# Stretched routing steps, whole-row second matrices of four experts and outputs in columns of 256, 128 and 128, in an attention, GLU and soft-MoE kernel

## The chip, the cores and the metric

The kernel runs on one core of one Trainium2 chip. The metric is the device time of one execution in microseconds (us); less is better. The time of the kernel before is the median of three executions.

## The reference

```python
def reference(**kw):                       # cut; all arrays float32
    # windowed causal attention: 4 batches, 8 heads, 576 positions, head width 64, window 64
    scores = where(0 <= i - j < 64, q @ k.T / sqrt(64), -1e9)
    x = softmax(scores) @ v                # -> x: 2304 tokens x 512
    # gated linear unit, no activation: w_a, w_b 512 x 1536, w_out 1536 x 512
    x = ((x @ w_a) * (x @ w_b)) @ w_out
    # soft mixture of 8 experts, 4 slots each (32 slots)
    logits = x @ phi                       # 2304 x 32
    d = softmax(logits, axis=0)            # over the tokens
    c = softmax(logits, axis=1)            # over the slots
    slot_in = d.T @ x                      # 32 x 512
    for e in range(8):
        slot_out[e] = maximum(slot_in[e] @ w1[e], 0) @ w2[e]   # w1 512 x 1024, w2 1024 x 512
    return c @ slot_out                    # 2304 x 512
```

## The kernel before

The 2304 tokens are 18 tiles of 128. For every tile the kernel runs attention, then the two GLU products, then the routing; `w_out @ phi` is multiplied out ahead (`project_phi`), so that routing needs only the GLU's product g (128 x 1536) and the output matrix is applied to the 32 slot inputs alone. Slot inputs are summed over the tiles with a running maximum (`stats`, `acc`).

**GLU.** `glu(t, fg, nm)` computes for tile t one third (fg = 0, 1, 2; 512 columns) of x @ w_a ("a") or x @ w_b ("b"). Activations and weights are split into a high and a low part, so each of four rows blocks takes three matmuls. For fg 0 and 1 that is 12 matmuls of 512 columns. For fg 2 the weights are staged by column halves (`stage_w`, `split_w`, `w_part`), and a unit is 24 matmuls of 256 columns. ScalarE copies the "a" sums from the PSUM bank into a buffer `asb`, and VectorE multiplies "b" from PSUM with it into g. There is one bank for "a" and one for "b".

**Slots.** The order on TensorE (PE) is written by hand. The first 24 slots (four tiles' GLU, their attention, the decoding of the weights) follow the table STARTUP. From then on `run_slot(n)` puts one GLU half ("a" in an even slot, "b" in an odd one) into slot n, and ahead of it everything that `at(n, ...)` has put there. There are 114 slots; in the last twelve, tiles 15, 16 and 17 run through fg 2 in column halves. The other engines' orders are made by a scheduler that follows the program and readiness.

**Routing steps of tile t**, placed relative to a slot R[t] (lines 752 to 782): `r_b` (for tiles 2 to 14) transposes a third of g in blocks of 32 on VectorE and brings it into shape by four DMAs to DRAM (gd) and one back (gT), all on SyncE's queue; `r_l` (slot R) multiplies it with wphi, giving the logits lps, copied to l; `r_k` (R+1) transposes l (lt), VectorE takes the maximum, ScalarE the exponential e; `r_d` (R+2) transposes e on PE (dps), copied to dt; `r_u` (R+3) multiplies dt with g (ups) and VectorE adds it to acc. R grows by 4 slots a tile while routing is behind the GLU, which needs 6 slots a tile; from tile 8 on it has caught up and grows by 6. The attention steps of tile t stand at fixed slots: `att_s` at sA[t] (scores, 16 maxima on VectorE, 8 exponentials on ScalarE), transposes of the probabilities two slots later, `att_pv` six slots later.

```python
        R[t] = max(done[t, NFG - 1] + (4 if t in by_squares else 3), R[t - 1] + 4 if t else 24)
...
            at(r, r_l, t)
            at(r + 1, r_k, t)
            at(r + 2, r_d, t)
            at(r + 3, r_u, t)
```

**Experts.** The weights w_out, w1 and w2 are fetched by `fetch` on SyncE's queue into a ring of buffers, 256 or 512 KB a DMA, in the order in which they are used; a buffer is filled again once the matmuls that read it are done. Experts 0 to 3 are half u = 0, experts 4 to 7 half u = 1; four experts share the PE by columns of 32. `h` (L905) is the first product, `ops` (L939) the second. `ops` runs over columns 0 to 255 for u = 0 and 1, then over columns 256 to 511 for both (PARTS). After each column part `slots_keep` copies the sums, `slots_pick` (so, L957) gathers the slots, `slots_split` makes the high and low part sor on ScalarE and VectorE, and `tokens_out` (op, L977) multiplies the token weights cT with sor: nine groups of two tiles per part, evacuated in turn by ScalarE and VectorE (ob), each written to DRAM by one DMA of 256 KB. Six groups of the first part alternate with `ops` of the second.

```python
        slots_out(1, 0, range(MF - EARLY))
        for j in range(EARLY):
            slots_out(1, 0, range(MF - EARLY + j, MF - EARLY + j + 1))
            tokens_out(0, j)
```

Of the kernel before, what the change touches and what calls it, by code (L numbers as in the profile page):

```python
# [11 lines left out]
F32 = mybir.dt.float32  # L12
# [28 lines left out]
    Da2.1 Sa2.3 Gb2.0 Gb2.0 Ri0 Tq5 Po1 Sb2.1 Ga2.1 Av3 Da2.0 Ga3.0 Da2.1 Da2.0 Po0 Ga3.0 Da2.2 Gb2.0 Da2.0  # L41
    Da2.2 An4.0 Po4 Po3 Gb1.1 Po1 Da2.0 Da2.2 Sb2.0 Gb1.1 Tv4 Da2.1 Gb1.1 Ga3.0 Po5 Da2.3 Da2.2 Po7 Ga3.0 Da2.2
    Po7 Da2.3 Gb1.1 Po7 Da2.2 Po4 An4.1 Tq5 Da2.1 Da2.2 Ga3.0 Po7 Da2.3 An4.1 Ga0.2 Gb1.1 Po0 Da2.3 Po7 Ap4.0
    Ga0.2 Ga0.2 Gb2.1 Po4 Ga0.2 Da2.3 Db2.0 Da2.3 Po4 Sb2.2 Db2.0 Po7 Da2.3 Po0 Ap4.0 Po5 Ga0.2 Gb2.1 An4.1 Po4
    Gb2.1 Gb2.1 Ga0.2 Ga0.2 Db2.0 Po0 Ga0.2 Po3 Po7 Po0 Db2.0 Po0 Ga0.2 Po6 Ga1.2 Po5 Db2.0 Po5 Ga1.2 Ga1.2 Po3
    Ga1.2 Po3 Po5 Po7 Po5 Ga1.2 Po0 Db2.2 Gb2.1 Ga1.2 Po2 Db2.0 Po5 Db2.2 Po0 Po5 Po3 Ga1.2 Db2.1 Db2.1 Db2.2
    Po7 Po7 Gb3.0 Ga1.2 Db2.0 Ga1.2 Db2.1 Gb3.0 Po2 Po7 Db2.2 Gb3.0 Po0 Db2.1 Ga3.1 Db2.2 Po5 Gb3.0 Po6 Ga3.1
    Sb2.3 Po7 Po2 Gb3.0 Po5 Po5 Ga3.1 Db2.1 Po2 Po6 Db2.2 Db2.1 Po2 Po2 Po6 Ga3.1 Ap4.1 Ga3.1 Db2.2 Po6 Po6 Po2
    Db2.3 Gb3.1 Ga2.2 Ga2.2 Po5 Gb3.1 Gb3.1 Po5 Po8 Po0 Db2.1 Ak5 Gb3.1 Ga2.2 Db2.3 Po9 Db2.3 Po0 Db2.3 Po0 Ak5
    Ga2.2 Ga2.2 Po6 Po0 Gb3.1 Ap4.1 Po8 Ga2.2 Po2 Gb0.2 Ak5 Gb0.2 Ga2.2 Db2.3 Av4 Po8 Po8 Po8 Po2 Gb0.2 Po2  # L50
    Ga2.2 Po8 Db2.3 Gb0.2 Po11 Db2.3 Gb0.2 Po2 Gb0.2 Po6 Tv5 Po2 Gb0.2 Po10 Gb0.2 Ga2.2 Tv5 Po2 Po8 Ga3.2 Po9
    Gb0.2 Po6 Ga3.2 Ga3.2 Po6 Po11 Gb1.2 Gb1.2 Po6 Ga3.2 Po9 Po8 Gb1.2 Gb1.2 Ga3.2 Gb1.2 Ga3.2 Po6 Po11 Po9 Po8
# [15 lines left out]
def swa_glu_softmoe_kernel(  # L68
# [34 lines left out]
    EARLY = 6  # L103
    N_EX3 = 1
    PARTS = ((0, 256), (256, 256))
# [25 lines left out]
    turns = {"as": [0, 2], "gT": [0, 2]}  # L131
# [257 lines left out]


    def stage_w(nm, fg, j):
        src = moe_w_a if nm == "a" else moe_w_b
        if fg == 0:
            pool, tag = wp, "w1"
        elif fg == 1:
            pool, tag = wp, "w3" if nm == "a" else "w2"
        elif nm == "a":
            pool, tag = wp, "w3" if j < 2 else "w2"
# [4 lines left out]
        if fg < NFG - 1:  # L403
            src = src[P * j:P * j + P, 512 * fg:512 * fg + 512]
            nc.sync.dma_start(out=st, in_=src.bitcast(I32).rearrange("p (f w) -> p f w", w=2))
        else:
            h, c = divmod(j, 2)
            src = src[256 * c:256 * c + 256, 512 * fg + 256 * h:512 * fg + 256 * h + 256]
            nc.sync.dma_start(
                out=st.rearrange("p (i f) w -> p i (f w)", i=2),  # L410
                in_=src.bitcast(I32).rearrange("(i p) f -> p i f", p=P),
            )

    def split_w(nm, fg, j):
# [3 lines left out]
        if i == 0:  # L418
            tag = f"w{fg + c}" if fg == NFG - 1 else f"w{fg}"
# [7 lines left out]
    def w_part(w, nm, fg, kk, h):  # L427
        if fg < NFG - 1:
            return w[nm, fg, kk // 2][:, kk % 2]
        return w[nm, fg, h][:, kk // 2, 256 * (kk % 2):256 * (kk % 2) + 256]  # L430

# [3 lines left out]
    def glu(t, fg, nm, halves=None):  # L435

        if t not in gts:
            gts[t] = gp.tile([P, DFF], F32, tag="g", name="g")
        xhi, xlo = xts[t]
        if fg < NFG - 1:  # L440
            parts = [(0, slice(0, 512))]
        else:
            parts = [(h, slice(256 * h, 256 * h + 256)) for h in (halves or range(2))]
        ps = ps_ab.tile([P, 512], F32, tag=nm, name=f"ps{nm}")
        for h, cols in parts:
            n = 0
            for kk in range(KD):
                wh, wl = w_part(whi, nm, fg, kk, h), w_part(wlo, nm, fg, kk, h)
                for l, r in ((xhi, wh), (xhi, wl), (xlo, wh)):
                    nc.tensor.matmul(ps[:, cols], lhsT=l[:, kk], rhs=r, start=(n == 0), stop=(n == 3 * KD - 1))  # L450
                    n += 1
                yield
        cols = slice(parts[0][1].start, parts[-1][1].stop)
        if nm == "a":
# [191 lines left out]
    def keep_c(t0, tags):  # L646
# [15 lines left out]
    order2 = [  # L662
        ("2", n, u, mh, e)
        for n, (_, nw) in enumerate(PARTS) for u in range(2) for mq in range(MF * nw // 1024)
        for e in range(4) for mh in (2 * mq, 2 * mq + 1)
    ]
    order += order2
# [5 lines left out]
    def source(key):  # L673

        if key[0] == "o":
            return wo_dram, (P * key[1], P), (0, DM), key[1] % 2 == 0
        if key[0] == "1":
            _, u, kk, e, n = key
            return moe2_w1[4 * u + e], (P * kk, P), (512 * n, 512), n == 0
        _, n, u, mh, e = key  # L680
        n0, nw = PARTS[n]
        nm = 512 // nw
        return moe2_w2[4 * u + e], (P * nm * mh, P * nm), (n0, nw), mh % 2 == 0

    def fetch(n=0):

        while nxt[0] < len(order):
# [17 lines left out]
            while h < nh and nxt[0] < len(order):  # L705
                key = order[nxt[0]]
                src, (r0, nr), (c0, ncol), pair = source(key)
                two = pair and h + 1 < nh
                if key[0] == "1":
                    ncol *= 1 + two  # L710
                else:
                    nr *= 1 + two
                nh2 = 1 + two
# [323 lines left out]
```

## Time and profile before

| | us |
|---|---|
| median of three executions | 549.45 |
| lowest, highest | 549.14, 549.58 |
| profiled execution: its own time | 547.72 |
| profiled execution: span on the core | 545.9 |
| PE busy in the span | 499.8 (92%) |
| VectorE busy | 314.6 (58%) |
| ScalarE busy | 200.9 (37%) |

The profile is of one execution. Its span runs from the first instruction to the last, and 1.8 us lie around it. PE is matmul, PEld weight load, DVE VectorE, ACT ScalarE, POOL GpSimd, SPq SyncE's DMA queue. A float32 matmul appears in the trace as two MATMUL records, one of the split GLU (fp32r) as one. Shapes are partitions by columns. Overlapping matmuls make the busy time of PE a poor measure of its speed; the spacing of starts, as the chain of waits gives it, is a better one. The granted clock of PE is at its full level, 2.4 GHz, from 95 us to the end of the matmuls but for the last stretch.

### The profile page before, as it was taken

Reading aid. Unit: us, or ns where it says so; the run is one execution under the profiler, and the core shown is the slowest. Engines: PE = TensorE matmul, PEld = TensorE weight load, DVE = VectorE, ACT = ScalarE, POOL = GpSimd, SP = SyncE. Lnnn points to the kernel's source line nnn. Section 1 sums busy time; section 2 is a strip of 40 time slices with the busy share of each in tenths; the row PEclk is TensorE's granted clock in tenths of the full one; section 3 lists DMA queues with packets and bytes.
Section 4 is the critical chain, followed back from the end, with each engine's and each line's share of the span. In section 5 each row is a group of like instructions: output and inputs, shape, how many; then the busy total and the mean of one; then the engine's idle time right before and its main releaser. Section 6 shows DMA issues by size and latency. Waiting matters only on the chain.

```text
span 545.9 us, 11859 instructions
## 1 busy us (share of the span) xinstructions
PE 499.8 (92%) x4471; PEld 388.9 (71%) x4471; DVE 314.6 (58%) x900; ACT 200.9 (37%) x624; POOL 119.9 (22%) x182
## 2 busy tenths in 40 slices
PE   4489788999999999999998897989999999989993
PEld 3367566789878888787887776777888778933452
DVE  3999999996537476473755536375763211143123
ACT  5667575455534233232432413143432211132013
POOL 3555456441001120211202020211241000020000
PEclk9999999999999999999999999999999999999998
DMA  9987269565326768767574655657769899699997
GB/s 271 260 234 228 68 216 282 175 182 162 103 59 162 186 152 218 209 149 184 156 193 117 156 163 127 171 122 182 200 162 282 320 372 384 247 348 348 349 356 250
DMA packets 143129, 116.06 MB, mean 213 GB/s; under 512 B 81888, under 2 KB 122848, under 8 KB 143072
## 3 DMA queue, kind: packets, MB, share of 16 engines
q1 hardware_dynamic: 137888, 99.58, 62.5%
q0 software_dynamic: 5184, 15.73, 10.0%
q8 instruction: 35, 0.57, 0.4%
q14 instruction: 22, 0.18, 0.1%
HBM read 90.90 MB, written 24.38 MB: 211 GB/s over the span
## 4 chain that ended last, share of the span: by engine, by line
PE 70%; DVE 18%; issue 3%; DMA 3%; ACT 3%; SPq 1%; POOL 0%; POOLq 0%; ACTq 0%
PE psb L450 26%; PE psa L450 20%; PE ops L939 3%; PE xps L348 3%; DVE w L375 3%; PE lps L503 3%; PE h L905 2%; DVE pr L273 2%; PE ups L579 2%; DVE w L379 2%; DMA gT<-gd 2%; DVE w L369 2%; PE s L260 2%; PE tg L140 1%; DVE w L371 1%
## 5 line engine op out<-in xcount | busy, mean ns | idle before, releaser
L450 PE MATMUL psb<-whb,x 128*128 128x512 f32 (+1 forms) x576 | 162.2, 350 | 1.7 <-DVE g L460 1.7
L450 PE MATMUL psa<-wha,x 128*128 128x512 f32 (+1 forms) x576 | 160.3, 347 | 2.6 <-ACT wha L423 1.6
L450 PEld LDWEIGHTS psa<-wha,x 128*128 128x128 f32 x576 | 101.4, 189 | 21.8 <-issue 6.0
L450 PEld LDWEIGHTS psb<-whb,x 128*128 128x128 f32 x576 | 101.8, 191 | 20.9 <-issue 7.1
L450 PE MATMUL psb<-wlb,x 128*128 128x512 f32 (+1 forms) x288 | 97.4, 338 | 0.9 <-POOL wlb L425 0.9
L450 PE MATMUL psa<-wla,x 128*128 128x512 f32 (+1 forms) x288 | 97.0, 337 | 1.2 <-POOL wla L425 1.2
L460 DVE TENSOR_TENSOR g<-psb,asb 128x512 f32<-128x512 f32 (+1 forms) x57 | 37.7, 661 | 94.0 <-PE psb L450 91.3
L456 ACT COPY asb<-psa 128x512 f32<-128x512 f32 (+1 forms) x57 | 31.9, 560 | 118.8 <-PE psa L450 118.3
L280 ACT ACTIVATE pr<-pr,nmx 128x128 f32<-128x128 f32 x144 | 55.9, 390 | 17.3 <-DVE nmx L273 17.3
L450 PEld LDWEIGHTS psa<-wla,x 128*128 128x128 f32 x288 | 54.7, 190 | 6.6 <-POOL wla L425 1.7
L450 PEld LDWEIGHTS psb<-wlb,x 128*128 128x128 f32 x288 | 55.0, 191 | 5.5 <-POOL wlb L425 1.2
L314 POOL DMA_DIRECT2D pd<-pq x48 | 26.4, 558 | 120.4 <-DVE cst L565 48.0
L351 ACT CAST x<-xps 128x512 fp32r<-128x512 f32 x18 | 10.5, 586 | 53.9 <-PE xps L348 53.9
L260 PE MATMUL s<-kTs,qTs 64*64 64x128 f32 x576 | 24.0, 303 | 6.0 <-DVE nmx L273 3.1
L478 DVE STREAM_TRANSPOSE gq<-g 128x512 f32<-128x512 f32 x39 | 27.4, 705 | 2.2 <-DMA gd<-gq 1.7
L280 ACT ACTIVATION_READ_ACCUMULATOR pr<-pr,nmx 128x1 f32 x144 | 27.0, 188 | 0.0
L320 POOL DMA_DIRECT2D pT<-pd x24 | 18.0, 756 | 40.0 <-DMA pd<-pq 32.0
L273 DVE CUSTOM_DVE_ANT_0 pr<-s,masks 128x128 f32<-128x128 f32 x112 | 24.8, 285 | 0.7 <-PE s L260 0.7
L260 PEld LDWEIGHTS s<-kTs,qTs 64*64 64x64 f32 x576 | 18.4, 148 | 9.4 <-issue 4.5
L234 POOL COPY kTs<-kTs 128x256 f32<-128x256 f32 x17 | 8.2, 480 | 73.9 <-DVE kTs L245 69.0
L245 DVE COPY kTs<-tk 128x512 f32<-128x512 f32 x13 | 9.0, 690 | 22.7 <-PE tk L140 22.7
L369 DVE TENSOR_SCALAR w<-w 128x512 f32<-128x512 f32 x24 | 16.3, 679 | 8.9 <-ACT w L367 8.9
(138 smaller groups left out, 725.9 us busy)
## 6 DMA issues: line engine op xcount, KB each, us to landing
xw<-in_moe_w_dram SPq DMA_DIRECT2D x39, 512.0 KB, 6.5
xw<-in_moe_w_dram SPq DMA_DIRECT2D x50, 256.0 KB, 6.0
gd<-gq SPq DMA_DIRECT2D x156, 64.0 KB, 2.7
gT<-gd SPq DMA_DIRECT2D x39, 256.0 KB, 3.3
st<-in_moe_w_b_dram SPq DMA_DIRECT2D x12, 512.0 KB, 5.8
st<-in_moe_w_a_dram SPq DMA_DIRECT2D x12, 512.0 KB, 5.8
st<-in_moe_w_out_dram SPq DMA_DIRECT2D x12, 512.0 KB, 4.8
pd<-pq POOLq DMA_DIRECT2D x48, 128.0 KB, 3.2
```

The costliest lines, as they stand in the source:

```text
L260: nc.tensor.matmul(sps[h][c, u], lhsT=qT[r, u, c], rhs=kTs[r, t % 2, u, W * b:W * b + P],)
L273: nc.vector.tensor_tensor_reduce(out=pr[:, u].rearrange("p (a k) -> p a k", a=2), in0=sps[h][:, u].rearrange("p (a k) -> p a k", a=2), in1 ...
L280: nc.scalar.activation(out=pr[:, u], in_=pr[:, u], func=ACTF.Exp, scale=-1.0, bias=nmx[:, i:i + 1], accum_out=sm[:, i:i + 1],)
L314: nc.gpsimd.dma_start(out=pd[:, :, i].rearrange("j k e -> k j e"), in_=pq[32 * i:32 * i + 32].rearrange("p j h u q -> p j (h u q)"),)
L320: nc.gpsimd.dma_start(out=pT, in_=pd[:, :, :, P * h:P * h + P].rearrange("j k i e -> (j k) i e"))
L348: nc.tensor.matmul(o, lhsT=vt[:, 2 * u + h, :], rhs=r)
L369: nc.vector.tensor_scalar(out=t, in0=t, scalar1=DBL_LO, scalar2=DBL_HI, op0=ALU.max, op1=ALU.min)
L375: nc.vector.scalar_tensor_tensor(out=i, in0=hi, scalar=-(1 << 30), in1=i, op0=ALU.bitwise_and, op1=ALU.bitwise_or)
L450: nc.tensor.matmul(ps[:, cols], lhsT=l[:, kk], rhs=r, start=(n == 0), stop=(n == 3 * KD - 1))
L456: nc.scalar.copy(out=asb[:, cols], in_=ps[:, cols])
L460: nc.vector.tensor_tensor(out=gts[t][:, gcols], in0=ps[:, cols], in1=pas.pop((t, fg))[:, cols], op=ALU.mult)
L478: nc.vector.transpose(out=gq.rearrange("p (j c t) -> p c j t", j=4, c=4), in_=gts[t][:, 512 * fg:512 * fg + 512].rearrange("p (c j f) -> p ...
```

## The change

Six things, in the order of the diff:

1. fg 2 of the GLU is staged, split and multiplied in whole rows like the other two: 12 matmuls of 512 columns instead of 24 of 256. For the last three tiles the order is a, a, a, b, b, b; there are 108 slots, the last six as long as the last twelve were. In STARTUP the surplus entries of fg 2 are dropped and two staging entries change places.
2. "a" is copied straight into g and multiplied there; `asb` stays for one unit (tile 4, fg 0).
3. Events may stand at half slots: `run_slot` puts them between the sixth and the seventh of the 12 matmuls.
4. Where the next tile's R is six slots away (tiles 7 to 12), routing is stretched: r_k at R+2, r_d at R+4, r_u at R+5, and R itself is one slot later from tile 8 to 13. Where it is catching up (tiles 1 to 6) and for tiles 13 and 14, r_d moves from R+2 to R+2.5. r_b of tiles 2 to 7 comes one slot earlier.
5. w2 of experts 0 to 3 is fetched in whole rows (four rows, 8 KB, to a partition, 4 KB of them in one DMA row), all 512 columns for u = 0 at once; w2 of experts 4 to 7 stays in halves of 256 columns. hT is transposed with a stride of four to match.
6. The outputs leave in columns 0 to 255, 256 to 383 and 384 to 511: nine groups of two tiles, then twice five groups of four tiles (the fifth of two). `ops` of u = 1 runs over 256, 128 and 128 columns; five groups alternate with the second part, seven with the third.

```diff
-    Da2.1 Sa2.3 Gb2.0 Gb2.0 Ri0 Tq5 Po1 Sb2.1 Ga2.1 Av3 Da2.0 Ga3.0 Da2.1 Da2.0 Po0 Ga3.0 Da2.2 Gb2.0 Da2.0
+    Da2.1 Sa2.3 Gb2.0 Gb2.0 Ri0 Tq5 Po1 Sb2.2 Ga2.1 Av3 Da2.0 Ga3.0 Da2.1 Da2.0 Po0 Ga3.0 Da2.2 Gb2.0 Da2.0
...
-    EARLY = 6
     N_EX3 = 1
-    PARTS = ((0, 256), (256, 256))
+    PARTS = ((0, 256), (256, 128), (384, 128))
...
+        ps = ps_ab.tile([P, 512], F32, tag=bank, name=f"ps{nm}")
+        n = 0
+        for kk in range(KD):
+            wh, wl = (w[nm, fg, kk // 2][:, kk % 2] for w in (whi, wlo))
+            for l, r in ((xhi, wh), (xhi, wl), (xlo, wh)):
+                nc.tensor.matmul(ps, lhsT=l[:, kk], rhs=r, start=(n == 0), stop=(n == 3 * KD - 1))
+                n += 1
+            yield
+        g = gts[t][:, 512 * fg:512 * fg + 512]
+
         if nm == "a":
-            asb = p2.tile([P, 512], F32, tag=turn("as"), name="asb")
-            nc.scalar.copy(out=asb[:, cols], in_=ps[:, cols])
-            pas[t, fg] = asb
-        else:
...
+            pas[t, fg] = p2.tile([P, 512], F32, tag="as1", name="asb") if (t, fg) == (NFIRST, 0) else g
+            nc.scalar.copy(out=pas[t, fg], in_=ps)
+        else:
+            nc.vector.tensor_tensor(out=g, in0=ps, in1=pas.pop((t, fg)), op=ALU.mult)
...
-        R[t] = max(done[t, NFG - 1] + (4 if t in by_squares else 3), R[t - 1] + 4 if t else 24)
+        R[t] = max(done[t, NFG - 1] + (3 if t not in by_squares else 4 if t == NTILE - NLAST - 1 else 5), R[t - 1] + 4 if t else 24)
...
-                    at(max(done[t, fg] + 1, r - (6, 4, 3)[fg]), r_b, t, fg)
+                    at(max(done[t, fg] + 1, r - (7, 5, 4)[fg]), r_b, t, fg)
...
+            o = (2, 4, 5) if t + 1 < NTILE - NLAST and R[t + 1] - r > 5 else (1, 2.5 if t else 2, 3)
             at(r, r_l, t)
-            at(r + 1, r_k, t)
-            at(r + 2, r_d, t)
-            at(r + 3, r_u, t)
+            at(r + o[0], r_k, t)
+            at(r + o[1], r_d, t)
+            at(r + o[2], r_u, t)
...
     def run_slot(n):
-        for f, a in events[n]:
+
+        for f, a in events[2 * n]:
             run(f, *a)
-        if n < NSLOT:
-            t, fg, *h = units[n // 2]
-            run(glu, t, fg, "ab"[n % 2], *h)
+        pieces = iter(glu(*halves[n], "ab"[n % 2]) if n < NSLOT else ())
+        for _ in range(KD // 2):
+            next(pieces, None)
+        for f, a in events[2 * n + 1]:
+            run(f, *a)
+        for _ in pieces:
+            pass
...
+    slots_out(0, range(MF))
     slots_keep(0, 0)
     with tc.manual_schedule(engines=MANUAL):
-        slots_out(0, 1, range(MF))
+        slots_out(1, range(MF), 0)
+        slots_out(1, range(1), 1)
         slots_keep(0, 1)
         slots_split(0)
-        slots_out(1, 0, range(MF - EARLY))
-        for j in range(EARLY):
-            slots_out(1, 0, range(MF - EARLY + j, MF - EARLY + j + 1))
-            tokens_out(0, j)
+        slots_out(1, range(1, 3), 1)
         slots_keep(1, 0)
-        slots_out(1, 1, range(MF))
-        tokens_out(0, EARLY)
+        for m in range(3, MF):
+            slots_out(1, range(m, m + 1), 1)
+            tokens_out(*todo.pop(0))
+        slots_out(1, range(1), 2)
         slots_keep(1, 1)
         slots_split(1)
-        for j in range(EARLY + 1, NOUT):
-            tokens_out(0, j)
-        for j in range(NOUT):
-            tokens_out(1, j)
+        slots_keep(2, 0)
+        for m in range(1, MF):
+            slots_out(1, range(m, m + 1), 2)
+            tokens_out(*todo.pop(0))
+        slots_keep(2, 1)
+        slots_split(2)
+        for n, j in todo:
+            tokens_out(n, j)
```

On ScalarE, around the routing of a tile that has caught up (pr are attention's exponentials, e, co and ce routing's, asb or g<-psa the copies of "a"), before:

```order
L351 CAST x<-xps 128x512
L280 ACTIVATE pr,sm<-pr,nmx 128x128 x8
L537 ACTIVATE e,es<-lt,nm 128x128
L543 ACTIVATE co<-nm 128x1
L456 COPY asb<-psa 128x512
L561 ACTIVATE ce,rsum<-lt,rm 128x32
L456 COPY asb<-psa 128x512
L226 ACTIVATE qTs<-tq 128x512
L456 COPY asb<-psa 128x512
```

and now:

```order
L348 CAST x<-xps 128x512
L277 ACTIVATE pr,sm<-pr,nmx 128x128 x8
L436 COPY g<-psa 128x512
L515 ACTIVATE e,es<-lt,nm 128x128
L521 ACTIVATE co<-nm 128x1
L539 ACTIVATE ce,rsum<-lt,rm 128x32
L436 COPY g<-psa 128x512
L223 ACTIVATE qTs<-tq 128x512
L436 COPY g<-psa 128x512
```

The exponential e now stands one copy of "a" further behind attention's eight exponentials, since r_k is placed two slots after them instead of in their slot.

On PE, the end of the program (ops is the second product of the experts, so the gathering of slots, op the output groups), before:

```order
L939 MATMUL ops<-xw,hT 32x256 x4
L977 MATMUL op<-sor,cT 128x256 x2
L939 MATMUL ops<-xw,hT 32x256 x32
L977 MATMUL op<-sor,cT 128x256 x2
L957 MATMUL so<-o,sel 128x128 x4
L977 MATMUL op<-sor,cT 128x256 x22
```

and now:

```order
L929 MATMUL ops<-xw,hT 32x128 x4
L966 MATMUL op<-sor,cT 128x256 x2
L929 MATMUL ops<-xw,hT 32x128 x4
L966 MATMUL op<-sor,cT 128x128 x4
L929 MATMUL ops<-xw,hT 32x128 x4
L966 MATMUL op<-sor,cT 128x128 x4
L929 MATMUL ops<-xw,hT 32x128 x4
L966 MATMUL op<-sor,cT 128x128 x4
L946 MATMUL so<-o,sel 128x128 x2
L966 MATMUL op<-sor,cT 128x128 x24
```

Eleven groups now stand ahead of the last `ops` instead of six, and seven groups behind the last `so` (two of them waiting for nothing of it, five for its 128 columns) instead of eleven.

## Rows read from the trace of the kernel before

**Rows 1.** Busy time of each engine in two stretches, with counts, PE's clock, DMA share

```profile
core 0: us, PE busy (x) PEld busy (x) DVE busy (x) ACT busy (x) POOL busy (x), PEclk, DMA share, GB/s
...
281.00:375.00 94.00, 85.92 (x799) 70.46 (x801) 48.76 (x166) 26.72 (x103) 15.64 (x27) 1.00 0.57 145
375.00:479.00 104.00, 103.61 (x895) 85.34 (x884) 42.82 (x143) 29.65 (x97) 12.24 (x20) 1.00 0.84 276
```

**Rows 2.** What PE waited for from 88 to 480 us: total, times, longest

```profile
PE dps L140 <- ACT ce L561: 6.4, 4, 1.6
...
PE lps L503 <- DMA gT<-gd: 1.6, 2, 1.3
...
PE lps L503 <- DVE dt L571: 0.4, 1, 0.4
```

**Rows 3.** Timeline of tile 8's routing: start, duration, engine, instruction, [idle before]

```profile
287.00 0.39 ACT L280 ACTIVATE pr<-pr,nmx 128x128 f32<-128x128 f32 x1
...
287.39 0.35 ACT L537 ACTIVATE e<-lt,nm 128x128 f32<-128x128 f32 x1
...
288.81 0.33 PE L140 MATMUL dps<-ident,e 128*128 128x128 f32 x1 [1.60 <-ACT ce L561]
```

**Rows 4.** Timeline of SyncE's queue, 293 to 305 us

```profile
298.94 0.60 SPq L206 DMA_DIRECT2D ldq<-in_q_dram  x1
299.70 0.50 SPq L489 DMA_DIRECT2D gT<-gd  x1
```

**Rows 5.** Chain that ended last, GLU halves: start, us, what, records

```profile
251.36 2.77 PE psa L450 x12
...
289.14 2.86 PE psb L450 x24
...
295.75 2.72 PE psb L450 x12
```

**Rows 6.** PE's groups by form, 110 to 479 us; first and last of 256 columns

```profile
L450 PE MATMUL psb<-whb,x 128*128 128x256 f32 x288 | 59.5, 291 | 0.0
...
L450 PE MATMUL psa<-wla,x 128*128 128x256 f32 x128 | 36.2, 282 | 0.0
```

**Rows 7.** Chain that ended last, 470 us to the end

```profile
472.59 0.44 PE tg L140 x4
...
474.45 0.35 PE lps L503 x8
...
504.03 7.00 PE h L905 x62
...
512.78 7.04 PE ops L939 x126
519.82 1.34 PE so L957 x8
...
522.59 0.43 PE op L977 x2
523.02 0.57 PE ops L939 x8
...
528.02 4.07 PE ops L939 x64
...
536.36 2.15 DMA out_dram<-ob
```

**Rows 8.** Timeline from 518 us: SyncE's output DMAs, PE's last groups

```profile
525.92 16.19 SPq L983 DMA_DIRECT2D out_dram<-ob  x18
...
535.19 2.92 PE L977 MATMUL op<-sor,cT 128*128 128x256 f32 x18 [1.10 <-DVE sor L966]
```

**Rows 9.** DMA rate and packet sizes, 497:525, 442:457 and 284:287 us

```profile
DMA packets 10049, 9.76 MB, mean 349 GB/s; under 512 B 570, under 2 KB 10045, under 8 KB 10045
...
DMA packets 1606, 5.83 MB, mean 388 GB/s; under 512 B 183, under 2 KB 183, under 8 KB 1606
...
DMA packets 2209, 0.67 MB, mean 224 GB/s; under 512 B 1697, under 2 KB 2209, under 8 KB 2209
```

More of the change, by code (lines that the diff above doesn't have):

```diff
@@ L425, in split_w, with glu @@
         nc.gpsimd.tensor_tensor(out=lo, in0=w32, in1=hi.bitcast(F32), op=ALU.subtract)
[L427 to L430, printed above, removed]
     gts = {}
     pas = {}
-    def glu(t, fg, nm, halves=None):
+    def glu(t, fg, nm, bank):
         if t not in gts:
@@ L661, in swa_glu_softmoe_kernel @@
     order += [("1", u, kk, e, n) for u in range(2) for kk in range(KD) for e in range(4) for n in range(2)]
[L662 to L665, printed above, removed]
+    order += [("2", 0, m, e) for mq in range(MF // 2) for e in range(4) for m in (2 * mq, 2 * mq + 1)]
+    order += [
+        ("2", n, mh, e) for n in (1, 2) for mq in range(MF // 4) for e in range(4) for mh in (2 * mq, 2 * mq + 1)
     ]
-    order += order2
     slots = []
@@ L675, in source @@
         if key[0] == "o":
-            return wo_dram, (P * key[1], P), (0, DM), key[1] % 2 == 0
-        if key[0] == "1":
[L678 to L683, printed above, removed]
+            src = wo_dram.rearrange("(c p) d -> p c d", p=P)
+            return src[:, key[1]:key[1] + 1], src[:, key[1]:key[1] + 2] if key[1] % 2 == 0 else None
+        if key[0] == "2" and key[1]:
+            _, n, mh, e = key
+            src = moe2_w2[4 + e].rearrange("(h p i) d -> h p i d", p=P, i=4)[mh // 2][:, :, 256 * n - 256:256 * n]
+            c = 2 * (mh % 2)
+            return src[:, c:c + 2], src if c == 0 else None
+        if key[0] == "1":
+            _, u, kk, e, c = key
+            src = moe2_w1[4 * u + e, P * kk:P * kk + P]
+        else:
+            _, _, m, e = key
+            src = moe2_w2[e].rearrange("(h p i) d -> h p (i d)", p=P, i=4)[m // 4]
+            c = m % 4
+        one, two = (src[:, 512 * c:512 * min(c + i, src.shape[1] // 512)].rearrange("p (o d) -> p o d", o=1) for i in (1, 2))
+        return one, two if c % 2 == 0 else None
     def fetch(n=0):
@@ L705, in fetch @@
             while h < nh and nxt[0] < len(order):
[L706 to L713, printed above, removed]
+                one, two = source(order[nxt[0]])
+                nh2 = 2 if two is not None and h + 1 < nh else 1
+                src = two if nh2 == 2 else one
                 nc.sync.dma_start(
-                    out=x[:, 512 * h:512 * (h + nh2)].rearrange("p (c d) -> p c d", d=ncol),
-                    in_=src[r0:r0 + nr, c0:c0 + ncol].rearrange("(c p) d -> p c d", p=P),
+                    out=x[:, 512 * h:512 * (h + nh2)].rearrange("p (c d) -> p c d", d=src.shape[2]), in_=src
                 )
@@ L788, in swa_glu_softmoe_kernel @@
     for n, f, t, *x in (
[L789 removed]
+        (-1.5, r_t, a, 2), (-1, r_l, a, (2,)), (-.5, r_k, a), (-.5, r_t, b, 2),
         (0, r_d, a), (0, r_l, b, (2,)), (0, r_t, c, 2), (0, r_u, a), (1, r_k, b), (1, both, 0, "gT0"),
```

111 lines of the change are left out of this document (43 added, 68 removed).

## The prediction

> **What bounds the kernel now.** I first read the busy times in two middle stretches [rows 1]: from 375 to 479 us PE (TensorE) works 103.61 of 104 us, so nothing but fewer or cheaper PE instructions shortens that stretch; from 281 to 375 us it works only 85.92 of 94, so 8.1 us of waiting lie there. VectorE and ScalarE are busy for half of both stretches or less, so neither is the bound; what they do late is a matter of order. Then I read the list of what PE waited for [rows 2]: the two largest entries there that concern routing are dps (the transpose of the routing exponentials) behind ScalarE, 4 times 1.6, together 6.4 us, and lps (the logits) behind the DMA gT, 1.6 us. Together that is 8.0, the whole deficit. Last comes the chain that ended last: its GLU halves [rows 5], and its end [rows 7], where PE runs alone to 532.09 us (528.02 + 4.07) and 13.8 more us go by until the span ends at 545.9.
>
> **Wait for e, removed.** At tile 8 ScalarE finishes the last of attention's eight exponentials at 287.39, and only then runs e (0.35); PE waits 1.60 and transposes at 288.81 [rows 3]. The rows call the releaser "ce", a later instruction on the same queue, but the time fits e. Routing and scores share a slot there, and r_d follows too soon. The change puts r_k one slot later and r_d two slots behind r_k instead of one. By the order fences one "a" copy now stands between the eight exponentials and e. A slot is about 2.8 us [rows 5], so e gains some 2.8 us against its neighbours on PE and pays one copy, under 1.2 (an output's product, copy and issue together, [rows 7, 8]); it should be ready more than a microsecond before dps. Four waits of 1.6 go: **-6.4**.
>
> **Wait for gT, removed.** SyncE issues the read gT at 299.70, behind the load ldq at 298.94 [rows 4]. That load waits for a buffer which attention's transposes free, and all behind it on SyncE's queue waits too. The change puts r_l one slot later for tiles 8 to 13, 2.8 us, more than the longest of the two waits (1.3, [rows 2]). **-1.6**. The wait for dt (0.4, [rows 2]) is left where it is. What is late next: in a stretch without waits the weights' transfers, which are issued when buffers come free; DMA share is 0.57 there [rows 1], against 0.84 in the stretch that is saturated on PE all the same, so I take nothing for it.
>
> **GLU of fg 2.** 24 matmuls of 256 columns took 2.86 us, 12 of 512 took 2.72, in another half 2.77 [rows 5]. That is 0.09 to 0.14 a half, 0.12 taken. After 110 us the four groups of 256 columns have 288, 256, 144 and 128 records [rows 6], 816 or 34 halves. 34 x 0.12 = **-4.1** (-3.1 to -4.8). All of it is on PE's own time, which is the bound there. The Trainium skill, page "TensorE: Matmul & The Clock Gate", section "Wait — 56ns, not 53.3ns?", puts about 2.5 ns of overhead on a warm matmul beside its columns; by that 12 matmuls fewer give 0.03 a half. The trace disagrees: 2.86 / 24 is 119 ns and 2.72 / 12 is 227, so 256 columns cost over 5 ns more than half of 512.
>
> **In-place "a", staging, half slots.** The copy of "a" goes into g instead of a buffer and is as long as before. It must wait until the matmuls that read that g (ups of an earlier tile) are done; only at one unit is that near, and there the bank is wanted a slot later. Zero; bound 0 to +0.6. The startup table loses entries but keeps its work. Zero; some tenths either way.
>
> **New distance r_d to r_u.** For eight tiles (1 to 6, 13, 14) r_d now leaves only half a slot, 1.4 us, for the copy dt and for what VectorE has before it. Behind the waiting ups on PE stands the GLU, so a wait would cost its full length. VectorE is busy for under 52% [rows 1] and the one dt wait seen was 0.4 [rows 2]: zero taken, up to 1.6 a tile (the length of the waits that VectorE's and ScalarE's queues give elsewhere) for the rival below.
>
> **Whole rows of w2, experts 0 to 3.** Packets over 2 KB moved 388 GB/s, those of 1 to 2 KB 349 [rows 9]; half of w2 is 8.4 MB, 24.0 us at the one and 21.6 at the other. The weights would land up to 2.4 us earlier. PE hides that: it takes 126 records of 256 columns in 7.04 us and 62 of 512 in 7.00 [rows 7], as steadily as it can. Only the last 64, at 4.07 instead of 64 x 55.9 ns = 3.6, leave 0.5 to gain, and I let that stand in the next sum.
>
> **The tail.** Up to 519.82, where the first so starts, the work is the same [rows 7]: four experts' 512 columns now, two halves of 256 before. From there to the end of the last ops it took 12.27 us. Now it takes 64 records of 256 columns (u = 1, 3.6); 16 groups of 8 records of 128 columns; so twice, 1.34 and half of it, 0.67 (2.0 together); eleven output groups, nine at 0.43 [rows 7] and two of four 128-column products; and two short waits, for sor and for an output bank, 0.8 (1.10 was seen, [rows 8]). A group of 8 records of 128 columns is not in the trace. Its bounds are 0.22 (8 x 28 ns, half of 55.9) and 0.57 (the same with 256 columns, [rows 7]); I take the 0.35 of lps, eight short records in the same precision [rows 7]: 5.6. Four 128-column output products lie between 0.43 (two of 256) and 1.34 (so, four 128-column matmuls in eight records); I take 0.66, midway between 0.44 (four transposes, [rows 7]) and 0.86 (twice a pair of 256). Sum 3.6 + 5.6 + 2.0 + 3.9 + 1.3 + 0.8 = 17.2, **+4.9**.
>
> From the last ops to the end of the span 13.8 us went by: so, the wait for sor, op, copy, and nine outputs. The first landed 2.15 after its issue at 536.36 [rows 7]; 8 more at 0.75 (256 KB at 349 GB/s, [rows 9]) and 1.4 for the rest reach 545.9. Now there come one output group 0.66, so 0.67, sor 1.1, op with its copy up to the issue 1.2 (535.19 to 536.36, [rows 7, 8]), landing 2.15, only 3.5 more outputs, and 1.4. An output of 512-byte packets takes between 0.75 and 1.17 (224 GB/s, packets mostly smaller, [rows 9]); 0.86 taken, near the first, since its packets are at the edge of that mix: 3.0. Sum 10.2, **-3.6**. The tail as a whole: **+1.3** (from -1.5, with 0.22 a group and no wait, to some +6, with 0.57, a dear output product and 1.17). The Trainium skill, page "DMA: Bandwidth & Descriptors", section "Specifications", gives 512 bytes as the smallest transfer at full rate; by that the outputs cost 0.75 and the tail 0.4 less, which no row here shows.
>
> **Sum.** -6.4 - 1.6 - 4.1 + 1.3 = -10.8. The profiled execution took 547.72 with a span of 545.9; it would take 536.9 with 535.1. It is 1.7 below the median of the runs, 549.45, from which the same difference gives **538.6**.
>
> **Rivals.**
> - *Short matmuls cost as much as those of 256 columns.* So is 128x128 at 1.34 for eight records [rows 7]. Then 16 groups take 0.57 instead of 0.35, +3.5, and three output groups on the path 0.86 instead of 0.66, +0.6: **542.7**. Against it: 512 and 256 columns scale.
> - *The wait for e stays.* r_k moved, but the "a" copy that now stands ahead of e waits for a GLU half's end, and e with it; the change then does not do what it says. +6.4, **545.0**. Against it: dps moved by two slots, the copy by one.
> - *The GLU's matmuls follow the page's overhead.* 0.03 instead of 0.12 a half, 34 halves: 3.0 less gain, **541.6**. The rows [rows 5] speak against it, but they are three halves.
> - *Half a slot is too short (slower).* At each of eight tiles dt comes late, ups waits, and the GLU behind it. At 1.6 a tile +12.8, **551.4**; it passes the time of before at 1.35 and is measurably slower from 1.5 a tile. For it: VectorE's queue is in order, and the copy may stand behind attention's maxima. Against it: tiles 1 to 6 lie partly where PE waited little, and VectorE was free half of the time.
>
> **How the numbers follow.** Forecast 68%, short matmuls 14%, e stays 10%, page's overhead 4%, half a slot too short 4%. The forecast's own terms spread by about 3 either way (tail, GLU). The range from 535.5 to 543.0 holds the forecast, the short matmuls and the overhead, less some edges; what it leaves out is mostly the wait for e and the slower case. A measurement here tells 0.2%, 1.1 us, from no change: faster 0.94, same 0.02 (half slots at 1.25 to 1.5), slower 0.04.
>
> **What would show it.** Right: in the list of PE's waits dps behind ScalarE and lps behind gT are gone, and the stretch of tiles 7 to 13 has under 1 us of PE's idle time; all GLU halves are 12 records in 2.72 to 2.77; the last ops ends some 5 us later relative to the first so, and the span ends about 10 after it instead of 13.8, with outputs 0.8 to 0.9 apart at the end. Wrong: dps with 1.6 again, or ups behind dt several times; fg 2's halves as long as before; a group of 8 ops records at 0.5 or more; gaps of PE behind weights.

## The result

| | before | changed kernel |
|---|---|---|
| first measurement: ratio, interval | 1 | 0.9872, 0.9832 to 0.9913 |
| second measurement: median, us | 549.65 | 543.69 |
| second measurement: ratio, interval | 1 | 0.9888, 0.9868 to 0.9907 |
| span of a profiled execution, us | 545.9, 548.5 | 541.8 |

The changed kernel is faster by 1.1 to 1.3%, on 549.45 us that is 6 to 7 us; 10.8 were forecast. Some executions of the kernels with three output parts (4 of 11 of the changed kernel; none of before or of the kernels with two parts below) take some 8 us longer, with TensorE's granted clock at half at the end where one was profiled; the figures leave them out, except for a few in the ratios of glu_256, stretch_only and rows_1k. The profile shown is that of run after_again below.

The same two stretches as in [rows 1]:

```profile
core 0: us, PE busy (x) PEld busy (x) DVE busy (x) ACT busy (x) POOL busy (x), PEclk, DMA share, GB/s
281.00:375.00 94.00, 94.00 (x812) 74.00 (x804) 57.80 (x196) 31.98 (x121) 18.14 (x32) 1.00 0.69 171
375.00:479.00 104.00, 101.54 (x754) 75.18 (x751) 40.63 (x132) 27.84 (x87) 14.03 (x29) 1.00 0.86 285
```

What PE waited for from 88 to 480 us, as in [rows 2] (total, times, longest):

```profile
PE pp L588 <- ACT wphi L596: 2.4, 2, 2.1
PE psb L429 <- DVE g L438: 2.1, 2, 1.3
PE lps L481 <- ACT gT L450: 1.0, 1, 1.0
...
PE ups L557 <- DVE dt L549: 0.8, 2, 0.6
PE tk L137 <- DVE pT L328: 0.8, 1, 0.8
```

PE is busy for all 94 us of the stretch that had 8.1 us of waiting; the entries of dps behind ScalarE and of lps behind the DMA gT are gone. In their place stand smaller ones: pp (the w_out @ phi product, at 112.8 us) and, in the catch-up tiles, lps behind gT's copy and tk. The wait of psb was there before (1.7), and that of ups stands in the last three tiles, which the window up to 480 us only now reaches.

One place to cut the span in three is xs, the first product after the last routing. The timeline gives its first start by tile (count: duration, first and last start).

In before:

```profile
L875 PE MATMUL xs<-xw,uT x24: 592/592/617, 488.3 to 490.5; 128*32 128x512 f32 x24
```

In before run again:

```profile
L875 PE MATMUL xs<-xw,uT x24: 592/592/617, 490.6 to 492.8; 128*32 128x512 f32 x24
```

In the changed kernel:

```profile
L860 PE MATMUL xs<-xw,uT x24: 592/592/617, 479.4 to 481.6; 128*32 128x512 f32 x24
```

The chain of waits around 121 us gives the other, the attention product xps of the fifth tile (start, time).

In before:

```profile
121.33 1.08 PE xps L348 x32
```

In before run again:

```profile
122.32 1.08 PE xps L348 x32
```

In the changed kernel:

```profile
124.14 1.08 PE xps L345 x32
```

| us | start to xps | xps to xs | xs to the end | span |
|---|---|---|---|---|
| before | 121.3 | 367.0 | 57.6 | 545.9 |
| before, run again | 122.3 | 368.3 | 57.9 | 548.5 |
| changed kernel | 124.1 | 355.3 | 62.4 | 541.8 |
| forecast, against before | 0 | -12.1 | +1.3 | -10.8 |
| measured, against the two of before | +1.8 to +2.8 | -11.7 to -13.0 | +4.5 to +4.8 | -4.1 to -6.7 |

So the middle is as forecast in sum, and what is missing went at both ends, most of it in the tail.

### The profile page after: what moved, and what is told of

Read it like the earlier page. It is cut to its first block, busy times and chain, and to the rows that moved or that the text cites. A ratio compares the mean times of both kernels' runs of the same rounds, so it can differ in the third digit from the quotient of the medians.

```text
span 548.0 us, 11017 instructions
## 1 busy us (share of the span) xinstructions
PE 510.2 (93%) x4057; PEld 375.1 (68%) x4057; DVE 317.7 (58%) x898; ACT 201.2 (37%) x623; POOL 120.4 (22%) x182
## 4 chain that ended last, share of the span: by engine, by line
PE 70%; DVE 16%; DMA 8%; issue 3%; ACT 2%; SPq 0%; POOL 0%; POOLq 0%; ACTq 0%
PE psb L429 24%; PE psa L429 23%; DMA xw<-in_moe_w_dram 6%; PE xps L345 3%; DVE w L372 3%; PE op L966 3%; PE lps L481 3%; PE ups L557 2%; DVE w L376 2%; PE s L257 2%; DVE w L366 2%; DVE pr L270 2%; PE tg L137 1%; DVE w L368 1%; PE ops L929 1%
## 5 line engine op out<-in xcount | busy, mean ns | idle before, releaser
L429 PE MATMUL psb<-whb,x 128*128 128x512 f32 x432 | 154.9, 410 | 2.1 <-DVE g L438 2.1
L429 PE MATMUL psa<-wha,x 128*128 128x512 f32 x432 | 152.4, 406 | 1.6 <-ACT wha L412 1.6
L429 PEld LDWEIGHTS psb<-whb,x 128*128 128x128 f32 x432 | 81.9, 190 | 30.1 <-issue 10.2
L429 PEld LDWEIGHTS psa<-wha,x 128*128 128x128 f32 x432 | 81.7, 189 | 22.7 <-issue 3.9
L429 PE MATMUL psa<-wla,x 128*128 128x512 f32 x216 | 85.0, 393 | 1.0 <-POOL wla L414 1.0
L429 PE MATMUL psb<-wlb,x 128*128 128x512 f32 x216 | 84.8, 393 | 0.0
L438 DVE TENSOR_TENSOR g<-psb,g 128x512 f32<-128x512 f32 x53 | 36.5, 689 | 71.9 <-PE psb L429 68.9
L436 ACT COPY g<-psa 128x512 f32<-128x512 f32 x53 | 31.0, 585 | 94.8 <-PE psa L429 84.6
L257 PEld LDWEIGHTS s<-kTs,qTs 64*64 64x64 f32 x576 | 18.9, 151 | 10.7 <-issue 4.9
L414 POOL TENSOR_TENSOR wlb<-w,whb 128x512 fp32r<-128x512 f32 x12 | 17.8, 1480 | 19.6 <-ACT whb L412 19.5
L929 PE MATMUL ops<-xw,hT 128*32 128x128 f32 (+2 forms) x256 | 21.1, 432 | 1.0 <-DMA xw<-in_moe_w_dram 0.9
```

Source lines behind the costliest of these rows:

```text
L257: nc.tensor.matmul(sps[h][c, u], lhsT=qT[r, u, c], rhs=kTs[r, t % 2, u, W * b:W * b + P],)
L414: nc.gpsimd.tensor_tensor(out=lo, in0=w32, in1=hi.bitcast(F32), op=ALU.subtract)
L429: nc.tensor.matmul(ps, lhsT=l[:, kk], rhs=r, start=(n == 0), stop=(n == 3 * KD - 1))
L436: nc.scalar.copy(out=pas[t, fg], in_=ps)
L438: nc.vector.tensor_tensor(out=g, in0=ps, in1=pas.pop((t, fg)), op=ALU.mult)
L929: nc.tensor.matmul(ops[u][32 * e:32 * e + 32, c0:c0 + nw], lhsT=hTs[u][m // 4][:, m % 4, 32 * e:32 * e + 32], rhs=w, start=(m == 0), stop= ...
```

## Experiments

**The changed kernel again**, unchanged (after_again). 

> The changed kernel once more, unchanged. Its first profile had TensorE's granted clock at 0.50 from some 518 us to the end and at 0.5 to 0.9 in parts of the first 70 us, with a span of 548.0. Theory: at full clock the end is what the prediction worked out, the span 539 to 541, the last ops some 17 us after u = 0's 512 columns are done, and 10 to 11 us from there to the end. Rival: the tail is slow for its own reasons (short matmuls, weights late), and the span from the last ops on is 13 us or more at full clock as well.

 Measured: the span is 541.8, the ratio 0.9888. The first theory holds in part: from the last ops to the end it takes 541.8 - 531.1 = 10.7 us, but the last ops comes 19.5 us after u = 0's columns are done, not 17 (below), and the span is 0.8 above the expected range.

The first measurement's own profile shows where its time went. Two of its stretches, in the columns of the table of stretches above:

```profile
515.00:520.00 5.00, 3.79 (x46) 2.34 (x43) 1.30 (x4) 0.96 (x2) 0.00 (x0) 1.00 0.91 292
520.00:525.00 5.00, 5.00 (x41) 2.70 (x40) 1.38 (x2) 0.93 (x2) 0.00 (x0) 0.51 0.38 127
```

PE, at 2.4 GHz (1.00), stood still for 1.2 of 5 us, 0.9 of them waiting for the experts' last weights; then the granted clock fell to 0.50 (1.2 GHz) and stayed there until the end of the program. The profiles of stretch_only and glu_256 show the same fall, at 519.9 and 525.9 us, each time about when the last weights landed (520.3 and 525.3). Those of after_again, rows_1k, even_tokens and old_routing do not, though PE waits for these weights there too (1.0 to 1.9 us); in no_rows, which waits 5.1, the clock fell briefly (0.66 on average from 520 to 525) and rose again; and no profile of a kernel with two output parts shows a fall in this stretch before its last products are done. So the third part can bring this cost as well; that the wait brings the fall about is not shown.

**Old routing distances** (old_routing).

```diff
-        R[t] = max(done[t, NFG - 1] + (3 if t not in by_squares else 4 if t == NTILE - NLAST - 1 else 5), R[t - 1] + 4 if t else 24)
+        R[t] = max(done[t, NFG - 1] + (4 if t in by_squares else 3), R[t - 1] + 4 if t else 24)
...
-                    at(max(done[t, fg] + 1, r - (7, 5, 4)[fg]), r_b, t, fg)
+                    at(max(done[t, fg] + 1, r - (6, 4, 3)[fg]), r_b, t, fg)
...
-            o = (2, 4, 5) if t + 1 < NTILE - NLAST and R[t + 1] - r > 5 else (1, 2.5 if t else 2, 3)
+            o = (1, 2, 3)
```

> The changed kernel with routing at its old distances (r_k, r_d, r_u one, two and three slots after r_l, r_l and r_b at their old slots). Theory (the two waits were the whole routing part): the waits of dps for e return, four to six of 1.6 us, and one or two of lps for gT, so 7 to 9 us longer than the changed kernel (548 to 550 if that runs 541). Rival (the shorter GLU halves and the copy in place already move e and gT): less than 4 us longer, with few dps waits in the list.

 Measured: ratio 1.0057 (1.0035 to 1.0080), so 1.7% or 9.3 us longer than the changed kernel: all other edits together do not pay without this one. PE's waits from 88 to 480 us:

```profile
PE dps L137 <- ACT ce L539: 7.0, 4, 1.8
PE lps L481 <- DMA gT<-gd: 2.4, 4, 1.8
```

Both waits are back, 9.4 us. The chain at tile 8 shows e's place: attention's exponentials in two pieces (x10, x5), e behind them, then dps.

```profile
288.40 1.97 ACT pr L277 x10
...
290.64 0.96 ACT pr L277 x5
291.60 0.34 ACT e L515 x2
...
292.92 0.33 PE dps L137
```

From xps to xs this kernel takes 366.1 us (124.2 to 490.3) against 355.3, 10.8 more; 9.4 are the returned waits, the changed kernel's 1.8 (lps, tk, above) go the other way, so some 3 us are not waits. The chain of the changed kernel around tile 8 shows what they may be:

```profile
286.57 0.79 PE lps L481 x24
287.36 2.95 PE psa L429 x12
290.31 2.72 PE psb L429 x12
293.03 0.22 PE lt L501 x2
293.25 0.14 PE lt L503 x2
293.39 2.85 PE psa L429 x12
```

A GLU half right behind another takes 2.72, behind lt 2.85, behind lps 2.95. With the stretched steps lps follows attention's scores and fewer halves follow foreign work. By the spacing of starts from tile 10's attention product to tile 13's the halves take 1.1 us less and lps and lt 1.0 less; that this is the rest is read, not tried alone.

**Outputs in two parts** (two_parts).

```diff
-    PARTS = ((0, 256), (256, 128), (384, 128))
+    PARTS = ((0, 256), (256, 256))
...
+        slots_out(1, range(2), 1)
         slots_keep(1, 0)
-        for m in range(3, MF):
+        for m in range(2, MF):
             slots_out(1, range(m, m + 1), 1)
             tokens_out(*todo.pop(0))
-        slots_out(1, range(1), 2)
+        tokens_out(*todo.pop(0))
...
```

> The changed kernel with outputs in two parts of 256 columns as before (six groups ahead of the last ops, one between, eleven behind), everything else kept. Theory of the prediction (the third part costs 1.3 us net, 4.9 on TensorE against 3.6 gained at the outputs): 0 to 2 us shorter than the changed kernel. Rival (the weights arrive earlier now, and the end is bound by the outputs' transfers, so that the third part gains): 2 to 4 us longer than the changed kernel.

 Measured: ratio 0.9818 (0.9797 to 0.9840), 0.7% or 3.8 us below the changed kernel. From xs to the end it takes 58.5 us (480.6 to 539.0), 3.9 less than the changed kernel's 62.4 and 0.6 to 0.9 more than before. One theory named too small an effect, the other the wrong one: the third part is a loss, three times as large as worked out. PE's timeline of the changed kernel where its second column part runs:

```profile
515.58 1.46 PE L946 MATMUL so<-o,sel 128*128 128x128 f32 x8
...
518.45 0.41 PE L929 MATMUL ops<-xw,hT 128*32 128x128 f32 x4
519.46 0.41 PE L929 MATMUL ops<-xw,hT 128*32 128x128 f32 x2 [0.60 <-DMA xw<-in_moe_w_dram]
520.77 0.41 PE L929 MATMUL ops<-xw,hT 128*32 128x128 f32 x2 [0.90 <-DMA xw<-in_moe_w_dram]
521.10 0.51 PE L966 MATMUL op<-sor,cT 128*128 128x256 f32 x2
```

One group of eight ops records takes from 518.45 to 521.10, 2.65 us, where an undisturbed one takes 0.36 (chain below). It stops twice, and each time goes on when a transfer of weights has just landed (519.4 and 520.7 us in the trace). In two_parts the last weights stretch one group by 0.5 us. SyncE's issues show why, as the timeline groups them (start, time from the first to the end of the last, count).

In before:

```profile
504.82 20.71 SPq L714 DMA_DIRECT2D xw<-in_moe_w_dram  x27
```

In the changed kernel:

```profile
505.28 10.82 SPq L694 DMA_DIRECT2D xw<-in_moe_w_dram  x15
```

In two_parts:

```profile
504.82 11.62 SPq L694 DMA_DIRECT2D xw<-in_moe_w_dram  x16
```

The last weights are issued at 525.5, 516.1 and 516.4, that is 37.2, 36.7 and 35.9 us after xs, and land 5 to 6 us later (530.8, 521.4 and 521.8): all three kernels get them at nearly the same pace. In before the last ops ends at 532.09, 1.2 us behind the last landing, so stream and PE ran side by side. The weights come in pieces of 256 columns, and the second part uses half of each and so runs through the pieces at twice the pace: it catches up with the stream and waits, and then the whole third part is still to be done. The last ops ends 3 us after the last landing in two_parts and 9.7 us after it in the changed kernel.

**The third GLU block by halves** (glu_256): for tiles 4 to 17 each unit again in two halves of 256 columns.

```diff
+        for c in (slice(0, 256), slice(256, 512)) if fg == NFG - 1 and t >= NFIRST else ():
+            n = 0
+            for kk in range(KD):
...
+                    nc.tensor.matmul(ps[:, c], lhsT=l[:, kk], rhs=r[:, c], start=(n == 0), stop=(n == 3 * KD - 1))
```

> The changed kernel with the third GLU column block of tiles 4 to 17 multiplied again in two halves of 256 columns, 24 matmuls instead of 12, in 28 of the 36 halves; staging, order and slots kept. Theory (0.09 to 0.14 us a half by the rows of before): 2.5 to 3.9 us longer than the changed kernel. Rival (2.5 ns of overhead a matmul, 0.03 us a half): 0.8 us longer.

 Measured: ratio 0.9966 (0.9932 to 1.0000), too wide for the question; the trace tells more. From xps to xs 358.7 us (124.0 to 482.7) against 355.3, 3.4 us for 28 halves, 0.12 each. Its chain at tile 8, to be compared with 2.95 and 2.72 in the same places above:

```profile
287.61 0.79 PE lps L490 x24
288.40 3.07 PE psa L431 x24
291.48 2.88 PE psb L431 x24
```

**Only the stretched routing** (stretch_only): the catch-up edits undone.

```diff
-                    at(max(done[t, fg] + 1, r - (7, 5, 4)[fg]), r_b, t, fg)
+                    at(max(done[t, fg] + 1, r - ((7, 5, 4) if t >= 8 else (6, 4, 3))[fg]), r_b, t, fg)
...
-            o = (2, 4, 5) if t + 1 < NTILE - NLAST and R[t + 1] - r > 5 else (1, 2.5 if t else 2, 3)
+            o = (2, 4, 5) if t + 1 < NTILE - NLAST and R[t + 1] - r > 5 else (1, 2, 3)
```

> The changed kernel with only the stretched routing of tiles 7 to 13 kept: r_d of tiles 1 to 6, 13 and 14 back at two slots after r_l, r_b of tiles 2 to 7 back at its old slots. Theory: in the changed kernel PE waits 0.8 for tk (behind pT on VectorE, 162 us) and 1.0 for lps (behind gT, 171 us), and neither wait is there with old routing; both come from the catch-up edits, so this kernel is 1.5 to 2.5 us shorter than the changed kernel, with both waits gone and the stretch of tiles 8 to 13 as fast. Rival: the two waits come from the new staging order ahead of them, and this kernel is within 0.7 us of the changed one.

 Measured: ratio 0.9916 (0.9876 to 0.9955), an interval too wide to place it beside 0.9888; the time decides nothing. In its trace the waits of tk and of lps behind gT are gone, and from xps to xs it takes 353.8 us (124.8 to 478.6), 1.5 less than the changed kernel. Other traces repeat it: this stretch takes 354.1 and 353.8 us in two_stretch and two_keep (below), which have the same routing, and 355.3 to 356.2 in the five further kernels' traces with the catch-up edits and 512-column GLU matmuls (the first measurement's, two_parts, even_tokens, no_rows, rows_1k). So the edits to the catching-up tiles cost about 1.5 us and cure nothing.

**Both** (two_stretch), the two edits above together. 

> Both at once: outputs in two parts of 256 columns, and of routing only the stretched tiles. If the two are independent: 3.9 us (third part, by spans) and 1.5 to 2.5 (catch-up edits) below the changed kernel, 537 to 538.5. Rival: the weights of the experts, the last of which landed at 521.4 and 521.8 us in both forms of the tail, bind the end, and little of the second gain arrives: 539 to 540.

 Measured: ratio 0.9791 (0.9767 to 0.9815), median 537.27, span 535.4: as independent gains would give, and 1% below the changed kernel.

**Weights of experts 0 to 3 in packets of 1 KB.** A first form (no_rows) split each transfer in two.

```diff
...
+                        nc.sync.dma_start(
+                            out=xs.rearrange("p (c i d) -> p c i d", c=2, d=256)[:, cc], in_=src[:, cc]
+                        )
...
```

> The changed kernel with w2 of experts 0 to 3 fetched in packets of 1 KB (each 512 KB transfer as two of 256 KB, one for each half of the columns); matmuls, buffers and order kept. Theory of the prediction (hidden behind PE): within 0.7 us of the changed kernel. Rival (in the changed kernel PE waits 1.5 us for the weights of the last experts, so the stream is on the path): the weights land up to 2.4 us later and the kernel is 1.5 to 3 us longer, with PE's waits for xw at 3 us or more.

 Measured: ratio 0.9984 (0.9966 to 1.0003), 5.3 us longer than the changed kernel, PE's waits for xw 5.1 us. But it changed two things, since most of these transfers became 128 KB. A second form (rows_1k) keeps one transfer of 256 KB a row block and only lays its halves apart:

```diff
+            apart = all(k[:2] == ("2", 0) for k in order[nxt[0]:nxt[0] + nh])
+            xa = x.rearrange("p (c h d) -> p h c d", c=2, d=256)
...
+                    nc.sync.dma_start(out=xa[:, h], in_=src.rearrange("p o (c d) -> p (o c) d", d=256))
```

> The changed kernel with w2 of experts 0 to 3 fetched in packets of 1 KB, one transfer of 256 KB for each row block (as most are in the changed kernel). The run before it on this question fetched the same bytes in twice as many transfers of 128 KB, and between 486 and 504 us moved 252 to 263 GB/s and ended 5.4 us later; so it confounded packet size with the number of transfers. Theory now (packet size alone costs 348 against 371 to 388 GB/s over 8.4 MB): the last weights land 1 to 2.4 us later, PE's waits for xw grow from 1.5 to between 2.5 and 4, and the kernel is 1 to 2.4 us longer than the changed kernel. Theory of the prediction (hidden): within 0.7 us. Rival (most of the 5.4 us was packet size): 4 us longer or more.

 Measured: ratio 0.9930 (0.9894 to 0.9966), which overlaps the changed kernel's. In the trace xs to the end takes 62.2 us (478.1 to 540.3) against 62.4, PE waits 1.3 for xw instead of 1.5, and the last weights land 41.7 us after xs, in the changed kernel 41.9. DMA rates from 486 to 504 us:

In no_rows:

```profile
DMA packets 4969, 4.62 MB, mean 257 GB/s; under 512 B 491, under 2 KB 4966, under 8 KB 4966
```

In rows_1k:

```profile
DMA packets 6359, 6.30 MB, mean 350 GB/s; under 512 B 367, under 2 KB 6228, under 8 KB 6356
```

In the changed kernel:

```profile
DMA packets 4903, 6.33 MB, mean 352 GB/s; under 512 B 366, under 2 KB 3281, under 8 KB 4900
```

In this stretch the size of the packets (2 KB for the whole rows here, 1 KB in rows_1k) changes nothing, 350 against 352 GB/s; the number of transfers does. So by these traces the whole rows neither gain nor cost time, and no_rows alone would have told the opposite.

**More output groups ahead** (even_tokens): seven instead of five among the second part.

```diff
-            tokens_out(*todo.pop(0))
+            for _ in range(2 if m in (5, 6) else 1):
+                tokens_out(*todo.pop(0))
```

> The changed kernel with seven of the first nine output groups among the products of the second column part instead of five, and so two fewer of them among those of the third (two of the second part move up in their place). Theory (PE runs through the second part twice as fast as its weights come, since they are fetched in 256 columns and used 128 at a time): the two waits for xw, 1.5 us, shrink to about 0.6, and the last ops ends 0 to 1 us earlier; but two groups less stand behind the last so, so the wait for its sor shows, and the span changes by less than 0.7 us. Rival (the waits for weights are the whole of what the third part costs beyond the prediction): 1.0 to 1.5 us shorter.

 Measured: ratio 0.9867 (0.9841 to 0.9893), not to be told from 0.9888. xs to the end takes 61.4 instead of 62.4; the wait for xw falls to 1.0, that for sor rises from 0.2 to 0.9. From the first to the last start of ops it takes 27.5 us in both (503.3 to 530.8, 501.3 to 528.8): ops as a whole ends no earlier. But the edit could not do what it was meant for: PE waits within the fifth group of the second part's products (m = 4), and the two added output groups stand behind the sixth and the seventh. The wait is shorter because the last weights landed 41.1 us after xs instead of 41.9. So this run decides between neither theory, and filling the wait is left untried.

**Before again** (before_again). 

> The kernel before once more, for a second trace of its start: its first profile was 1.7 us below its median, and it reached the attention product of its fifth tile at 121.3 us, the changed kernel's traces at 122.0 to 125.2. Theory (the changed kernel's start is no slower, the first profile of before was a quick one): 122.5 us or more. Rival (the new staging order costs 2 to 3 us): 121.5 or less again.

 Measured: 122.3 at xps, span 548.5. That lies between the two expectations. The changed kernels' traces stand at 121.9 to 125.2 there, with pp waiting 0.4 to 2.5 us. In the changed kernel PE's clock was 0.91 from 105 to 125 us, after its wait of 2.1; in two_keep, where that wait was 0.4, it was 1.00 and xps came at 122.5. The traces of the changed kernel and its variants lie 1.7 us behind the two of before there on average; whether the new staging order costs that stays open.

**One group moved behind the last ops** (two_keep), on top of two_stretch.

```diff
             tokens_out(*todo.pop(0))
-        tokens_out(*todo.pop(0))
         slots_keep(1, 1)
```

> The fastest version so far (outputs in two parts, of routing only the stretched tiles) with the one output group that stands between the last ops and the copies for so moved behind them, so that three groups instead of two stand where PE waited 1.1 us for sor. Theory: the last so 0.4 to 0.9 us earlier, the wait for sor under 0.8, the span 0.5 to 1 us shorter. Rival: the outputs' transfers bind the end, and nothing changes (within 0.3 us).

 Measured: ratio 0.9771 (0.9741 to 0.9801), span 535.9 against 535.4. The wait for sor is gone, 0.7 for an output bank and 0.3 for o stand in its place. Nothing is gained, as the rival said, though xs to the end is 0.5 us longer and not within its 0.3; the DMA engines' share is 1.00 to 1.04 from 526 to 534 us, so the outputs' transfers do fill the end. two_stretch and two_keep are the fastest versions, 2.1 to 2.3% below before.

## Why the prediction came out as it did

**Direction** held, the size did not: 538.6 was forecast; the two ratios give 542.4 and 543.3 on 549.45, the one just inside and the other just outside the range's upper end of 543.0. The rival nearest in time, short matmuls at 542.7, is so by luck: its mechanism did not come (below).

**Routing: right in mechanism, a little under-sized.** Without the edit 10.8 us more pass between xps and xs (old_routing); the prediction had 8.0 from the two waits. They are back at 9.4 there; the 8.0 of [rows 2] was the smaller of two values, since before run again has 9.3 (its lps waits 2.9 for gT). Without these two waits the middle takes 359.0 us in both traces of before and 356.7 in old_routing, so all other edits together gave 2.3 there, 1 less than the GLU alone (3.4, glu_256); what took that 1 us stays open. It is in part luck that the middle's sum fits: the stretched steps gave more than was counted, and the rest and the catch-up edits less. The rival in which the wait for e stays did not come.

**GLU: right.** 0.12 a half was taken and 0.12 measured. The estimate of 0.03 worked out from the Trainium skill, page "TensorE: Matmul & The Clock Gate", section "Wait — 56ns, not 53.3ns?", would have given 0.8 us for glu_256; the trace shows 3.4, about 10 ns for each matmul more, so trace and page disagree here.

**Half a slot: the slower rival did not come.** The waits of ups for dt are 0.8 us in all, and those stand in the last three tiles as before. What the catch-up edits cost came from steps priced at nothing: lps behind gT 1.0 and tk 0.8 in tiles that catch up.

**Whole rows: zero was right, the reason was not.** The prediction had the weights land up to 2.4 us earlier and PE hide that. They landed no earlier (rows_1k): the 388 GB/s of [rows 9] belong to packets of mostly 4 KB, and the whole rows of the stretch from 486 us on came in packets of 2 KB. Nor is PE alone the bound there: the prediction looked at PE, which did not wait, and not at the last transfer, which landed 1.2 us before PE was done with it.

**The tail: the step that failed**, +1.3 forecast, +4.5 to +4.8 measured. Its small prices were good. The chain of the changed kernel:

```profile
525.24 0.36 PE ops L929 x8
525.59 0.43 PE op L966 x2
...
529.11 0.66 PE op L966 x4
529.77 0.35 PE ops L929 x8
530.13 0.59 PE op L966 x4
530.72 0.36 PE ops L929 x8
531.08 0.59 PE op L966 x4
```

Eight ops records of 128 columns take 0.35 to 0.36 (0.35 taken), four 128-column output products 0.59 to 0.66 (0.66 taken); short matmuls do not cost as much as those of 256 columns, so that rival falls too. The row of 2.65 us instead of 0.36 is 2.3 us of waiting and starting again for weights, which the sum had put at nothing; with it 17.2 becomes 19.5, and 19.5 was measured (from 511.6, four us ahead of so's first start at 515.58, to 531.08). Behind the last ops 10.7 came for 10.2. The outputs of 512-byte packets moved 288 GB/s at the end, those of 1 KB 341.

The changed kernel, 534 to 540 us:

```profile
DMA packets 3484, 1.73 MB, mean 288 GB/s; under 512 B 114, under 2 KB 3484, under 8 KB 3484
```

Before, 538 to 544 us:

```profile
DMA packets 2121, 2.05 MB, mean 341 GB/s; under 512 B 124, under 2 KB 2121, under 8 KB 2121
```

That is 0.91 us an output; 0.86 was taken. The Trainium skill, page "DMA: Bandwidth & Descriptors", section "Specifications", names 512 bytes as the smallest transfer at full rate; the trace does not agree, 288 against 341. Ahead of ops the transposes of h (th), which now read with a stride of four, take some 0.09 us longer for each group of four, four times, 0.4 us that the prediction had not seen. One such group in the chain of before:

```profile
501.88 0.59 PE th L140 x4
```

In that of two_parts, which reads the same way as the changed kernel:

```profile
494.40 0.68 PE th L137 x4
```

These three, 2.3 for the weights, 0.5 behind the last ops and 0.4 ahead, make up 3.2 of the 3.2 to 3.5 us by which the tail came out dearer than forecast.

The third part itself, tried alone, costs 3.9 us by the traces of two_parts: ops stretches by 7.5 us between its first and last start (27.5 against 20.0, 504.4 to 524.4), and some 3.5 come back behind it.

## What to carry to other kernels

Where a stream of weights and PE end within about a microsecond of each other, neither is hidden: read the landing of the last transfer and its last use, not only who waits. Cutting the last product into narrower columns shortens what stands behind it, but a pass over half of each fetched piece goes through the pieces twice as fast; count its waits, and the work that is left behind the last landing. A step that is late by a fixed order was cured here by distance where there was room (tiles 7 to 13); where there was none, moving it cured nothing.

## What the runs showed of the hardware

- In the chain of the changed kernel a GLU half of twelve matmuls took 2.72 us behind another half, 2.85 behind two transposes and 2.95 behind the logits' short matmuls; interleaving costs PE time even without a wait.
- A stream mostly of 128 KB transfers, with a DMA instruction every 0.5 us, moved 257 GB/s from 486 to 504 us; transfers of 256 KB with the same 1 KB packets moved 350.
- Outputs in packets of 512 bytes left at 288 GB/s, in packets of 1 KB at 341, with the DMA engines busy throughout both times.
- Transposes that read with a stride of four columns took 0.68 us for four, 0.59 without.
- In three profiles TensorE's granted clock fell from 1.00 to 0.50 for the last 26 to 28 us, next to a wait of PE for weights of 0.9 us or more; in four others with such a wait it stayed at 1.00 until PE's work was done.
